# Linear attention with a gated feed-forward layer on one core: how the reciprocal denominators get from 72 partitions to 128

## The chip, the core and the metric

The kernel runs on one core of one Trainium2 chip. The metric is the device time of one execution in microseconds (us), the median of three runs. The engines are TensorE (PE in the profile, with PEld for its weight loads), VectorE (DVE), ScalarE (ACT), GpSimd (POOL) and SyncE (SP), whose queue issues all of this kernel's transfers.

## What is computed

The reference has two parts. Cut to what matters:

```python
def phi(x):                                    # x: batch 8, heads 8, 576 positions, 64 dims
    proj = einsum('bhsd,df->bhsf', x, w_phi)   # 128 features
    proj = proj - max(abs(proj), axis=-1)
    return concatenate([exp(proj), exp(-proj)], axis=-1)
q_p, k_p = phi(q), phi(k)
kv  = einsum('bhsf,bhsd->bhfd', k_p, v)
z   = sum(k_p, axis=2)
num = einsum('bhsf,bhfd->bhsd', q_p, kv)
den = einsum('bhsf,bhf->bhs', q_p, z)[..., None] + 1e-06
x = num / den                                  # 512 wide per position, all heads side by side
h = maximum(x @ w_in, 0)                       # 1024 wide
h_out = (h * sigmoid(conv(h, conv_w, 3 taps along the positions))) @ w_out
```

The change concerns one step of it, the division `num / den`.

## The kernel before, in words

The work is done batch by batch (b = 0 to 7). The eight heads of a batch are four pairs (p = 0 to 3), and a pair lies on 128 partitions: 64 dims of one head above 64 dims of the other. For each pair of pairs (qd = 0, 1) and each of five groups of positions (g = 0 to 4) there is a chain for k and a chain for q.

- `k_process` loads k and v, splits k into two float32r parts (`kxh`, `kxl`, on POOL), projects (`kp`), takes the maximum (`km`) and subtracts it (`ks`) on DVE, exponentiates on ACT (`ke`) and accumulates `kv` on PE.
- `q_process` does the like for q (`qxh`, `qxl`, `qp`, `qm`, `qs`), transposes (`tp`), exponentiates (`qh`, `qe`, `ql`), and multiplies with `kv` (`nm`). The product has 65 rows: 64 of the numerator and one of the denominator. ACT copies the numerators to `num` (128 x 576 for a pair) and the denominator row to `dr`; a transfer spreads `dr` over 72 partitions of 16 numbers each (`den`, line 377).
- `x_process` divides, once for each pair. DVE adds 1e-6 and takes the reciprocal (`rc`, 72 x 16, lines 392 and 393). Four transfers of line 397 bring each head's 576 reciprocals to two single partitions of the constant tile `rr` (partitions 0 and 32 for one head, 64 and 96 for the other). Then, for each of two halves c of the positions (290 wide, overlapping at the middle), a DVE stream shuffle spreads partition 0 of each block of 32 over its block (`xf`, line 405), a DVE multiplication forms num / den (line 406), ACT rounds it to float32r (`xh`) and DVE takes the rest (`xl`, both by way of `split`, lines 60 and 65).
- `h_part` and `o_part` are the feed-forward layer: `hp` (line 429) multiplies `xh`, `xl` with `win_hi`, `win_lo`; ACT applies relu (`h`); `conv_process` makes the three-tap convolution, the sigmoid and the gate on POOL, DVE and ACT (`c`, `gh`, `gl`); `op` (line 488) multiplies with `wout_hi`, `wout_lo`, and the output is stored from `os`.
- In the first part of the run the weights are loaded too: `w_r` holds 64-bit floats, and DVE, ACT and POOL turn them into float32r pairs (`w_t`, lines 96 to 105).

The order of the instructions on each engine is not the order of the code. A planner at the end of the function decides in which sequence the chains are recorded, and after that a scheduler orders each engine's instructions by priority and by its own estimate of when operands are ready. So an edit in `x_process` moves instructions on every engine. On each engine, and on SP's queue, instructions then run strictly in that order: one that waits holds up all behind it.

Of the kernel before, what the change touches and what calls it, by code (L numbers as in the profile page):

```python
# [7 lines left out]
F32 = mybir.dt.float32  # L8
# [4 lines left out]
ALU = mybir.AluOpType  # L13
AX = mybir.AxisListType.X

B, H, S, D = 8, 8, 576, 64
F = 128
DM, FF = 512, 1024
P = 128
NQ = 2  # L20
TC = 288
HW = TC + 2
# [13 lines left out]
def kernel(  # L36
# [13 lines left out]
    nc = tc.nc  # L50
    cp = ctx.enter_context(tc.tile_pool(name="cp", bufs=1))
    sb = ctx.enter_context(tc.tile_pool(name="sb", bufs=1))
    pg = ctx.enter_context(tc.tile_pool(name="pg", bufs=4, space=bass.MemoryType.PSUM))
    pm = ctx.enter_context(tc.tile_pool(name="pm", bufs=2, space=bass.MemoryType.PSUM))
    pk = ctx.enter_context(tc.tile_pool(name="pk", bufs=1, space=bass.MemoryType.PSUM))

    def split(src, hi, lo, eng_hi, eng_lo):

        if eng_hi is nc.scalar:
            nc.scalar.activation(out=hi, in_=src, func=AF.Copy)  # L60
        elif eng_hi is nc.gpsimd:
            nc.gpsimd.tensor_scalar(out=hi, in0=src, scalar1=1.0, scalar2=0.0, op0=ALU.mult, op1=ALU.add)  # L62
        else:
            nc.vector.tensor_copy(out=hi, in_=src)
        eng_lo.tensor_tensor(out=lo, in0=src, in1=hi.bitcast(F32), op=ALU.subtract)  # L65
# [12 lines left out]
    split(wbd_f, wbd_hi, wbd_lo, nc.vector, nc.vector)  # L78
    idn = load_const(ident, [P, P], "idn")


    rr = cp.tile([P, S], F32, name="rr")
    nc.gpsimd.memset(rr, 0.0)

# [66 lines left out]
    def pe(ns):  # L153
        return ("pe", ns)
# [4 lines left out]
    def until(*keys):  # L159
        return ("until", [k for k in keys if k is not None])  # L160

    def set_ready(key, ns=0):
        ready[key] = now[0] + ns * LAT
# [134 lines left out]
    xh, xl = {}, {}  # L298

    def q_process(b, qd, g):  # L300
# [80 lines left out]
        if g == 2 or g == 4:  # L381
            spawn(x_process(b, qd * 2 + g // 2 - 1))

    def x_process(b, p):
        yield ("wait", 4000)
        qd, pr = divmod(p, 2)
        dn, nt = den[b, qd, pr], numt[b, qd, pr]
        if 4 * b + p > 0:
            yield until(("x", *divmod(4 * b + p - 1, 4), 1))
        with tc.high_priority():  # L390
            rc = sb.tile([72, 16], F32, name=f"rc{b}_{p}", tag="rc", bufs=2)
            nc.vector.tensor_scalar(out=dn, in0=dn, scalar1=1e-6, scalar2=None, op0=ALU.add)
            nc.vector.reciprocal(out=rc, in_=dn)
            for i in range(2):
                for j in range(2):
                    row = D * i + 32 * j
                    nc.sync.dma_start(out=rr[row : row + 1, :].rearrange("o (r c) -> o r c", c=16),
                                      in_=rc.rearrange("(r i) c -> i r c", i=2)[i])
        yield ("wait", 4500)
        for c in range(2):  # L400
            yield until(("h", 2 * (b - 1) + c) if b > 0 else None)
            t0 = 0 if c == 0 else S - HW
            with tc.high_priority():
                xf = sb.tile([P, HW], F32, name=f"xf{b}_{p}_{c}", tag="xf", bufs=2)
                nc.vector.stream_shuffle(out=xf, in_=rr[:, t0 : t0 + HW], mask=[0] * 32)
                nc.vector.tensor_tensor(out=xf, in0=nt[:, t0 : t0 + HW], in1=xf, op=ALU.mult)
                xh[b, p, c] = sb.tile([P, HW], F32R, name=f"xh{b}_{p}_{c}", tag="xh", bufs=8)
                xl[b, p, c] = sb.tile([P, HW], F32R, name=f"xl{b}_{p}_{c}", tag="xl", bufs=8)
                split(xf, xh[b, p, c], xl[b, p, c], nc.scalar, nc.vector)
            set_ready(("x", b, p, c), 2500)  # L410
            yield pe(125)

# [145 lines left out]
    while moe is not None or chains or active:  # L558
        while chains and sum(1 for p in active if p[2]) < WINDOW:
            b, x, g, kind = chains.pop(0)  # L560
# [3 lines left out]
            p = active[-1]  # L564
# [10 lines left out]
        if can_a and (a_first or not can_m):  # L575
            p = active[can_a[0]]
# [66 lines left out]
```

## Time and profile before

| | |
|---|---|
| median of 3 runs | 825.59 us (824.98 to 825.75) |
| the profiled execution's own time | 825.6 us |
| its span, first to last instruction | 823.5 us |
| PE busy | 788.0 us, 96% of the span |
| DVE busy | 645.6 us, 78% |
| ACT busy | 569.5 us, 69% |
| POOL busy | 307.6 us, 37% |
| granted TensorE clock, mean | 0.989 |
| stream shuffles (line 405) | 64, 29.0 us of DVE |
| multiplications num / den (line 406) | 64, 32.0 us of DVE |
| transfers of line 397 | 128, of 2.2 KB each |

Busy shares are averages over the whole run. The kernel has a first part of about 140 us, in which weights are converted beside the first batches, and then a repeating part with a period of about 95.7 us for each batch; the two have to be read apart, by stretches of time. A row of the view by stretches has, for each engine, its busy us and in brackets the number of instructions, then the granted clock, the mean busy share of the 16 DMA engines and the GB/s they moved. A row of the view by lines has the line, engine, operation, tiles and shapes, the count, the busy us and the mean ns of one, and the idle time just before with what ended it.

### The profile page before, as it was taken

The page shows a single profiled execution, that of the slowest core. Times are in us where ns is not written, and L with a number is a line of the kernel's source. Part 1 is how long each engine was busy: PE and PEld are TensorE (multiplying, and loading weights), DVE is VectorE, ACT ScalarE, POOL GpSimd, SP SyncE. Part 2 cuts the span into 40 slices and gives each one's busy share as a digit, 9 for nine tenths or more (in the row PEclk, how much of TensorE's full clock was granted, in tenths as well). Part 3 has the DMA queues.
Part 4 walks back from the last instruction along what each step waited for, and adds up shares of the span by engine and source line. Part 5 has one row for each costly group of instructions (what it writes and reads, how often), then busy time and mean ns, then how long its engine had stood idle before and what let it go on. Part 6 is the DMA issues. An engine that isn't in the chain of part 4 may idle for free.

```text
span 823.5 us, 17817 instructions
## 1 busy us (share of the span) xinstructions
PE 788.0 (96%) x6350; PEld 772.5 (94%) x6350; DVE 645.6 (78%) x1390; ACT 569.5 (69%) x1228; POOL 307.6 (37%) x467
## 2 busy tenths in 40 slices
PE   7778779999999999999999999999999999999998
PEld 6767678999999999999999999999999999999998
DVE  4879999799987769787779878788697878766551
ACT  4598777797788867687586857678576867644332
POOL 4757765444443424414233333424334131111110
PEclk9799989999999999999999999999999999999999
DMA  6544421211211302121121211112021100000001
GB/s 187 157 134 135 135 66 47 67 41 44 70 56 44 93 18 71 27 82 50 46 61 43 69 34 60 47 50 82 15 77 29 56 12 19 13 30 30 23 23 44
DMA packets 56328, 49.18 MB, mean 60 GB/s; under 512 B 15024, under 2 KB 54192, under 8 KB 56240
## 3 DMA queue, kind: packets, MB, share of 16 engines
q1 hardware_dynamic: 56240, 48.05, 20.1%
q8 instruction: 51, 0.84, 0.4%
q14 instruction: 37, 0.30, 0.1%
HBM read 38.13 MB, written 9.44 MB: 58 GB/s over the span
## 4 chain that ended last, share of the span: by engine, by line
PE 74%; DVE 10%; ACT 7%; issue 4%; DMA 3%; POOL 1%; SPq 1%; DVEq 0%; ACTq 0%; POOLq 0%
PE op L488 22%; PE hp L429 21%; PE kv L255 8%; PE nm L356 8%; PE tp L320 3%; PE kp L199 2%; PE nm L348 2%; PE kp L200 2%; PE kp L201 2%; PE qp L199 1%; PE qp L200 1%; PE qp L201 1%; DMA w_r<-in_w_in_dram 1%; PE kv L251 1%; DVE qm L204 1%
## 5 line engine op out<-in xcount | busy, mean ns | idle before, releaser
L457 DVE SCALAR_TENSOR_TENSOR c<-h,cw,c 128x287 f32<-128x287 f32 (+1 forms) x256 | 138.7, 554 | 49.4 <-POOL c L452 47.5
L452 POOL TENSOR_SCALAR c<-h,cw 128x288 f32<-128x288 f32 x128 | 75.0, 588 | 243.6 <-ACT h L436 184.3
L255 PE MATMUL kv<-v,ke 128*128 128x65 f32 x1024 | 159.4, 255 | 1.4 <-ACT ke L236 1.2
L255 PEld LDWEIGHTS kv<-v,ke 128*128 128x128 f32 x1024 | 153.5, 193 | 4.8 <-ACT ke L236 1.8
L429 PE MATMUL hp<-xh,win_hi 128*128 128x290 f32 x512 | 153.2, 300 | 0.6 <-ACT os L493 0.6
L429 PE MATMUL hp<-xl,win_hi 128*128 128x290 f32 x512 | 152.7, 298 | 0.2 <-DVE xl L65 0.2
L488 PE MATMUL op<-gh,wout_hi 128*128 128x288 f32 x512 | 152.2, 298 | 0.0
L429 PE MATMUL hp<-xh,win_lo 128*128 128x290 f32 x512 | 151.9, 297 | 0.0
L488 PE MATMUL op<-gl,wout_hi 128*128 128x288 f32 x512 | 151.4, 296 | 0.0
L488 PE MATMUL op<-gh,wout_lo 128*128 128x288 f32 x512 | 150.9, 295 | 0.0
L436 ACT ACTIVATE h<-hp 128x290 f32<-128x290 f32 x128 | 52.2, 414 | 71.7 <-PE hp L429 71.2
L429 PEld LDWEIGHTS hp<-xh,win_hi 128*128 128x128 f32 x512 | 96.7, 190 | 1.5 <-ACT os L493 1.4
L62 POOL TENSOR_SCALAR kxh<-kr 128x256 fp32r<-128x256 f32 (+1 forms) x80 | 43.8, 547 | 144.1 <-PE kp L200 134.6
L429 PEld LDWEIGHTS hp<-xl,win_hi 128*128 128x128 f32 x512 | 97.0, 189 | 0.6 <-DVE xl L65 0.6
L429 PEld LDWEIGHTS hp<-xh,win_lo 128*128 128x128 f32 x512 | 97.1, 190 | 0.0
L488 PEld LDWEIGHTS op<-gh,wout_lo 128*128 128x128 f32 x512 | 96.4, 188 | 0.0
L488 PEld LDWEIGHTS op<-gl,wout_hi 128*128 128x128 f32 x512 | 96.2, 188 | 0.0
L488 PEld LDWEIGHTS op<-gh,wout_hi 128*128 128x128 f32 x512 | 96.1, 188 | 0.0
L65 DVE TENSOR_TENSOR ql<-qe,qh 128x512 fp32r<-128x512 f32 x112 | 79.9, 732 | 9.9 <-ACT qh L60 9.5
L236 ACT ACTIVATE ke<-ks 128x512 f32<-128x512 f32 (+1 forms) x80 | 46.9, 586 | 39.1 <-DVE ks L206 36.5
L326 ACT ACTIVATE qe<-tp 128x512 f32<-128x512 f32 x112 | 61.2, 595 | 12.2 <-PE tp L320 10.4
L356 PE MATMUL nm<-ql,kvh 128*65 128x256 f32 x224 | 68.4, 308 | 0.3 <-DVE ql L65 0.2
(84 smaller groups left out, 1989.5 us busy)
## 6 DMA issues: line engine op xcount, KB each, us to landing
v<-in_vt_dram SPq DMA_DIRECT2D x80, 130.0 KB
out_dram<-os SPq DMA_DIRECT2D x64, 144.0 KB
qr<-in_qT_dram SPq DMA_DIRECT2D x64, 128.0 KB
kr<-in_kT_dram SPq DMA_DIRECT2D x64, 128.0 KB
w_r<-in_w_in_dram SPq DMA_DIRECT2D x8, 512.0 KB
w_r<-in_w_out_dram SPq DMA_DIRECT2D x8, 512.0 KB
rr<-rc SPq DMA_DIRECT2D x128, 2.2 KB
qr<-in_qT_dram SPq DMA_DIRECT2D x16, 64.0 KB
```

Of the source, the lines that this page charges most:

```text
L62: nc.gpsimd.tensor_scalar(out=hi, in0=src, scalar1=1.0, scalar2=0.0, op0=ALU.mult, op1=ALU.add)
L65: eng_lo.tensor_tensor(out=lo, in0=src, in1=hi.bitcast(F32), op=ALU.subtract)
L199: nc.tensor.matmul(out=o, lhsT=his, rhs=wbd_hi, start=True, stop=False)
L236: nc.scalar.activation(out=e[:, 0], in_=pr, func=AF.Exp)
L255: ins = nc.tensor.matmul(out=kp[i][:, s, p0 : p0 + VW], lhsT=lhsT, rhs=v[:, (2 * t + i) * VW : (2 * t + i + 1) * VW], start=False, stop=(g ...
L326: nc.scalar.activation(out=e, in_=tp.rearrange("p i t s -> p i (t s)"), func=AF.Exp, scale=1.0 - 2.0 * s)
L356: ins = after(ins, lambda: nc.tensor.matmul(out=ps[:, i, o : o + w], lhsT=w_, rhs=x_, start=(k == 0), stop=(k == 5)))
L429: nc.tensor.matmul(out=ps, lhsT=w_, rhs=x_, start=(k == 0), stop=(k == 11))
L436: nc.scalar.activation(out=hs, in_=ps, func=AF.Relu)
L452: nc.gpsimd.tensor_scalar(out=cv, in0=hs[:, o : o + TC], scalar1=cw[:, f, 1:2], scalar2=0.0, op0=ALU.mult, op1=ALU.add)
L457: nc.vector.scalar_tensor_tensor(out=cv[:, lo:hi], in0=hs[:, o + j - 1 + lo : o + j - 1 + hi], scalar=cw[:, f, j : j + 1], in1=cv[:, lo:hi ...
L488: nc.tensor.matmul(out=ps, lhsT=w_, rhs=x_, start=(k == 0), stop=(k == 23))
```

## The change

The reciprocals take another way from the 72 partitions of `rc` to the 128 partitions of the pair. One transfer writes them to a tile `rd` in device memory, two rows of 576. A second transfer reads them back with each row repeated over 64 partitions into `rb` (128 x 576). The constant tile `rr`, its memset, the stream shuffles and the tile `xf` are gone. The multiplication with `num` is done once for the pair over all 576 positions, in place in `rb`, in the first of the two halves; both halves then split from slices of `rb`. `rb` and `rd` have two buffers each.

```diff
+    dp = ctx.enter_context(tc.tile_pool(name="dp", bufs=2, space=bass.MemoryType.DRAM))
...
-    rr = cp.tile([P, S], F32, name="rr")
-    nc.gpsimd.memset(rr, 0.0)
...
             nc.vector.reciprocal(out=rc, in_=dn)
-            for i in range(2):
-                for j in range(2):
-                    row = D * i + 32 * j
-                    nc.sync.dma_start(out=rr[row : row + 1, :].rearrange("o (r c) -> o r c", c=16),
-                                      in_=rc.rearrange("(r i) c -> i r c", i=2)[i])
+            rd = dp.tile([2, S], F32, name=f"rd{b}_{p}", tag="rd", bufs=2)
+            nc.sync.dma_start(out=rd.rearrange("i (r c) -> r i c", c=16), in_=rc)
+            rb = sb.tile([P, S], F32, name=f"rb{b}_{p}", tag="rb", bufs=2)
+            nc.sync.dma_start(out=rb, in_=rd.unsqueeze(1).broadcast_to([2, D, S]))
         yield ("wait", 4500)
         for c in range(2):
...
-                xf = sb.tile([P, HW], F32, name=f"xf{b}_{p}_{c}", tag="xf", bufs=2)
-                nc.vector.stream_shuffle(out=xf, in_=rr[:, t0 : t0 + HW], mask=[0] * 32)
-                nc.vector.tensor_tensor(out=xf, in0=nt[:, t0 : t0 + HW], in1=xf, op=ALU.mult)
+                if c == 0:
+                    nc.vector.tensor_tensor(out=rb, in0=nt, in1=rb, op=ALU.mult)
...
-                split(xf, xh[b, p, c], xl[b, p, c], nc.scalar, nc.vector)
+                split(rb[:, t0 : t0 + HW], xh[b, p, c], xl[b, p, c], nc.scalar, nc.vector)
```

The new code moves instructions. On DVE, the rows from the first pair's reciprocal (`rc_0`) to the first use of what the transfers bring (for batch 0; `w_t` are weights being converted, `km`, `ks`, `qm`, `qs` maxima and differences of the next groups). Before:

```order
L393 RECIPROCAL rc_0_829<-den_0_0_500 72x16
L98 TENSOR_SCALAR w_t<-w_r 128x512
L100 SCALAR_TENSOR_TENSOR w_t<-w_r,w_t 128x512
L204 TENSOR_REDUCE km_0_0_711<-kp_0_0_707 128x2
L103 SCALAR_TENSOR_TENSOR w_t<-w_t,w_r 128x512
L204 TENSOR_REDUCE qm_1_1_721<-qp_1_1_718 128x4
L206 TENSOR_TENSOR ks_0_0_713<-kp_0_0_707,km_0_0_711 128x256
L96 TENSOR_SCALAR w_t<-w_r 128x512
L206 TENSOR_TENSOR qs_1_1_723<-qp_1_1_718,qm_1_1_721 128x512
L204 TENSOR_REDUCE qm_1_2_736<-qp_1_2_733 128x4
L405 STREAM_SHUFFLE xf_0_0_948<-rr 128x290
```

The same place after the change, where the first use is the multiplication into `rb`:

```order
L391 RECIPROCAL rc_0_829<-den_0_0_500 72x16
L96 TENSOR_SCALAR w_t<-w_r 128x512
L98 SCALAR_TENSOR_TENSOR w_t<-w_r,w_t 128x512
L202 TENSOR_REDUCE km_0_0_711<-kp_0_0_707 128x2
L101 SCALAR_TENSOR_TENSOR w_t<-w_t,w_r 128x512
L202 TENSOR_REDUCE qm_1_1_721<-qp_1_1_718 128x4
L204 TENSOR_TENSOR ks_0_0_713<-kp_0_0_707,km_0_0_711 128x256
L403 TENSOR_TENSOR rb_0_834<-num_0_0_501,rb_0_834 128x576
L94 TENSOR_SCALAR w_t<-w_r 128x512
L204 TENSOR_TENSOR qs_1_1_723<-qp_1_1_718,qm_1_1_721 128x512
```

The first use has moved forward past three instructions: nine stood between it and the reciprocal, six stand there now. For the four pairs of batch 0 the numbers between are 9, 10, 9 and 13 before, and 6, 7, 7 and 12 now.

On PE, the place at which the first feed-forward products of batch 0 (`hp`, from `xh_0_0`) stand among the attention's products (`nm`, `kv`, `tp`, `kp`, `qp`). Before:

```order
L255 MATMUL kv_1_1_439<-v_1_4_599,ke_1_4_698 128x65 x2
L320 MATMUL tp_1_1_800<-idn,qs_1_1_723 128x128
L199 MATMUL kp_0_1_808<-wbd_hi,kxh_0_1_727 128x256
L200 MATMUL kp_0_1_808<-wbd_lo,kxh_0_1_727 128x256
L201 MATMUL kp_0_1_808<-wbd_hi,kxl_0_1_728 128x256
L199 MATMUL kp_0_1_808<-wbd_hi,kxh_0_1_727 128x256
L200 MATMUL kp_0_1_808<-wbd_lo,kxh_0_1_727 128x256
L201 MATMUL kp_0_1_808<-wbd_hi,kxl_0_1_728 128x256
L320 MATMUL tp_1_1_800<-idn,qs_1_1_723 128x128 x3
L196 MATMUL qp_1_3_822<-wbd_f,qr_1_3_760 128x256 x2
L348 MATMUL nm_1_0_850<-qh_1_0_704,kvh_1_0_794 65x64
```

(Nine more rows of `nm_1_0` and `kv_0` follow there before the first `hp`.) After the change:

```order
L346 MATMUL nm_0_4_764<-qh_0_4_684,kvh_0_1_436 65x256
L253 MATMUL kv_1_1_439<-v_1_4_599,ke_1_4_698 128x65 x2
L426 MATMUL hp_0_1578<-xh_0_0_949,win_hi_93 128x290
L426 MATMUL hp_1_1593<-xh_0_0_949,win_hi_93 128x290
L318 MATMUL tp_1_1_800<-idn,qs_1_1_723 128x128
L197 MATMUL kp_0_1_808<-wbd_hi,kxh_0_1_727 128x256
L198 MATMUL kp_0_1_808<-wbd_lo,kxh_0_1_727 128x256
L199 MATMUL kp_0_1_808<-wbd_hi,kxl_0_1_728 128x256
```

The first two `hp` products have moved ahead of `tp_1_1`, `kp_0_1`, `qp_1_3` and `nm_1_0`, which now stand behind them.

## The prediction

> **What bounds the kernel now.** I read the stretches of time first, because a mean over the run mixes two regimes. PE, PEld, DVE, ACT and POOL busy, then clock, DMA share, GB/s:
>
> ```profile
> span 823.5 us, 17817 instructions
> 57.00:140.00 83.00, 67.88 (x518) 61.05 (x517) 81.45 (x153) 64.23 (x139) 57.97 (x67) 0.96 0.35 104
> 175.00:250.00 75.00, 74.02 (x622) 73.79 (x623) 71.33 (x158) 60.83 (x130) 35.07 (x49) 1.00 0.18 50
> 300.00:395.70 95.70, 95.64 (x803) 95.22 (x800) 77.05 (x169) 69.12 (x150) 33.39 (x57) 1.00 0.19 53
> ```
>
> From 300 us on, one period of 95.70 us has 95.64 us of PE: nothing but PE counts there, and DVE is idle for 18.65 us of each period. Between 57 and 140 us it is the other way round: DVE is busy for 81.45 of 83 us and PE for 67.88, so PE loses 15.1 us there. That is where weights are converted on DVE beside the first batches, and where the four divisions of batch 0 lie. Between 175 and 250 us both are nearly full. So a saving or a delay on DVE counts at full price before 140 us, perhaps in part up to 250 us, and hardly at all after that.
>
> Then the waits, of PE and of DVE in 57 to 140 us (total, times, longest), with one row of the whole run's waits:
>
> ```profile
> PE tp L320 <- DVE ks L206: 4.0, 3, 3.4
> DVE w_t L96 <- POOL wout_lo L65: 0.8, 1, 0.8
> DVE xf L405 <- DMA rr<-rc: 15.6, 7, 3.7
> ```
>
> PE's longest wait there is on DVE. DVE's longest is 0.8 us, and none of the shuffles' waits for `rr` falls into that stretch: all seven (15.6 us) come later, where DVE has room. So the reciprocals' way through the transfers is hidden behind other DVE work today, and the question is whether it still is.
>
> **What the change takes off DVE.** The lines of DVE in 57 to 140 us:
>
> ```profile
> L65 DVE TENSOR_TENSOR ql<-qe,qh 128x512 fp32r<-128x512 f32 x10 | 10.6, 1070 | 0.0
> L206 DVE TENSOR_TENSOR ks<-kp,km 128x512 f32<-128x512 f32 (+1 forms) x12 | 7.3, 608 | 0.0
> L204 DVE TENSOR_REDUCE qm<-qp 128x4 f32<-128x512 f32 (+1 forms) x12 | 7.6, 630 | 0.0
> L103 DVE SCALAR_TENSOR_TENSOR w_t<-w_t,w_r 128x512 f32<-128x512 int32 x9 | 7.1, 789 | 0.0
> L406 DVE TENSOR_TENSOR xf<-num,xf 128x290 f32<-128x290 f32 x10 | 7.1, 748 | 0.0
> L100 DVE SCALAR_TENSOR_TENSOR w_t<-w_r,w_t 128x512 int32<-128x512 int32 x9 | 6.9, 771 | 0.0
> L204 DVE TENSOR_REDUCE km<-kp 128x4 f32<-128x512 f32 (+1 forms) x11 | 6.9, 624 | 0.0
> L98 DVE TENSOR_SCALAR w_t<-w_r 128x512 int32<-128x512 int32 x9 | 5.9, 651 | 0.3 <-ACT w_t L97 0.3
> L96 DVE TENSOR_SCALAR w_t<-w_r 128x512 int32<-128x512 int32 x9 | 5.1, 570 | 0.8 <-POOL wout_lo L65 0.8
> L405 DVE STREAM_SHUFFLE xf<-rr 128x290 f32<-128x290 f32 x10 | 4.3, 482 | 0.0
> ```
>
> For each pair two shuffles (2 x 482 ns) and two multiplications (2 x 748 ns) go, 2460 ns, and one multiplication of 576 columns comes. No row shows it. Between the 290 columns of line 406 (748 ns) and the 512 of `ql` (1070 ns) a column costs 1.45 ns, which gives 1163 ns at 576; its bounds are 1070 ns and twice 748 ns. I take 1163: 1.3 us saved for each pair, 5.2 us in batch 0 (3.9 to 5.6). The 28 later pairs save as much each, where PE doesn't wait for it: nothing, as long as DVE's idle time stays. The memset that goes ran on POOL before anything needed it, and the splits keep their sizes: nothing.
>
> **What the change makes of the transfers.** Before, four transfers are issued one behind the other, and the shuffle waits for the last. The chain of work that ended last shows such a case undisturbed, and early in the run a slow landing of a load (start, us, what):
>
> ```profile
> 8.01 2.57 DMA kr<-in_kT_dram
> ...
> 253.04 0.75 SPq L397
> 253.84 0.71 SPq L397
> 254.59 1.83 DMA rr<-rc
> ```
>
> An issue takes 0.7 to 0.8 us, and a transfer 1.83 us from its issue to landing; the four take 4.2 us. Now there are two that depend on each other: the write to `rd`, and the read, which SP may only issue when the write has landed. The write moves the same 72 rows of 64 bytes and I give it the same 1.83 us (no row shows it alone; the bounds are 1.83 and the 2.57 of the slow load). The read moves 128 rows of 2304 bytes, 295 KB, and its price hangs on how many of the 16 DMA engines carry it. For that, the packets of the page and all the issues (count, KB each):
>
> ```profile
> DMA packets 56328, 49.18 MB, mean 60 GB/s; under 512 B 15024, under 2 KB 54192, under 8 KB 56240
> v<-in_vt_dram SPq DMA_DIRECT2D x80, 130.0 KB
> out_dram<-os SPq DMA_DIRECT2D x64, 144.0 KB
> qr<-in_qT_dram SPq DMA_DIRECT2D x64, 128.0 KB
> kr<-in_kT_dram SPq DMA_DIRECT2D x64, 128.0 KB
> w_r<-in_w_in_dram SPq DMA_DIRECT2D x8, 512.0 KB
> w_r<-in_w_out_dram SPq DMA_DIRECT2D x8, 512.0 KB
> rr<-rc SPq DMA_DIRECT2D x128, 2.2 KB
> qr<-in_qT_dram SPq DMA_DIRECT2D x16, 64.0 KB
> kr<-in_kT_dram SPq DMA_DIRECT2D x16, 64.0 KB
> den<-dr SPq DMA_DIRECT2D x64, 2.0 KB
> den<-dr SPq DMA_DIRECT2D x32, 0.5 KB
> wbd_f<-in_wbd_dram SPq DMA_DIRECT2D x1, 128.0 KB
> idn<-in_ident_dram SPq DMA_DIRECT2D x1, 64.0 KB
> cw_raw<-in_conv_w_dram SPq DMA_DIRECT2D x1, 24.0 KB
> ```
>
> Data packets under 512 B are 128 x 36 of `rr`, 64 x 32 and 32 x 8 of `den` (64 bytes each) and the 128 of `cw_raw`: 7040. The other 7984 fit one closing packet from each engine that takes part. The issues are 547 transfers, so 16 engines for each would give 8752. The 768 that are missing are 128 x 4 + 32 x 8: the transfers of 36 rows use 12 engines and those of 8 rows use 8. So the engines are dealt out by the outermost count, as a divisor of it: 12 is the largest up to 16 that divides 36. The read has an outermost count of 128 on the side of `rb` and of 2 on the side of `rd` (two heads, each row then repeated 64 times). No transfer of before has two unequal sides, so 2 and 16 engines are both open, and this decides the forecast. I take 2, since an engine can only be dealt whole rows of the outer loop on both sides.
>
> The Trainium skill ("DMA: Bandwidth & Descriptors", "Why a DMA increments its semaphore by 16 and not by 1", and again in "Rules for kernel authors") states it so: the count is the largest up to 16 that divides the outermost size of both sides, and a broadcast with few copies outermost confines the whole transfer to so few engines. By that rule the change is slower; the trace agrees with it as far as the 12 and the 8 above.
>
> What one engine moves, from the densest stretch of weight loads:
>
> ```profile
> 35.00:37.00 2.00, 2.00 (x22) 2.00 (x20) 2.00 (x3) 0.48 (x1) 1.68 (x2) 1.00 0.71 251
> ```
>
> 251 GB/s over 0.71 x 16 engines is 22.1 GB/s for each. Half of 295 KB is 147.5 KB, 6.7 us on each of two engines; on 16 it would be 0.8 us. With 1.83 us for issue and landing the read takes 8.5 us, and write and read 10.4 us (2.7 and 4.5 us on 16 engines).
>
> From the Trainium skill's figure of about 27 GiB/s for an engine (the same page, "Specifications") one would estimate 5.1 us in place of 6.7, and a forecast lower by 6.4 us; no row here shows an engine at that rate.
>
> **What that costs.** The multiplication stands in DVE's queue where the order puts it: 6, 7, 7 and 12 instructions behind the reciprocal in batch 0, together 32. They are of the seven kinds of rows quoted above (570 to 789 ns), 0.66 us each in the mean, so 21.2 us of work. Four times 10.4 us less 21.2 us leaves 20.4 us in which DVE waits, about 6 us for each of the first three pairs and 2 for the fourth. Behind the multiplication wait `w_t`, `qs_1_1`, `qm_1_2` and `xl`, and behind those ACT and PE. On PE the first `hp` now stands ahead of `tp_1_1` and `kp_0_1` and holds them up until `xh_0_0` is there, so PE has no other work to turn to. On SP the read waits 1.1 us past the write's issue; queued behind it are `v_0_2`, `kr_0_4`, `qr_1_3` and a `den`. Each of these is on all 16 engines, so its share on the two slow ones lands up to 6.7 us later. I price that at nothing for batch 0, because DVE stands still in that time anyway; it is the reason for a rival below. SP itself issues 64 transfers fewer, and is idle enough for that to bring nothing.
>
> DVE in this stretch is idle for 1.55 us, which can be absorbed. The sum: -5.2 + 20.4 - 1.6 = +13.6 us. For batches 1 and 2 (42 and 43 instructions between) there are waits too, but PE is served ahead there. An instruction of 175 to 250 us is 71.33/158 = 0.45 us, so in batch 1 the waits are 41.6 - 18.9 = 22.7 us against 5 us saved and 3.7 us of idle. I take zero for it, with a bound of 14 us. The reason is this stretch around a shuffle that waited 3.7 us without PE losing more than 0.03:
>
> ```profile
> 250.00:260.00 10.00, 9.97 (x87) 9.81 (x85) 5.47 (x15) 7.97 (x18) 4.08 (x8) 1.00 0.26 70
> ```
>
> From batch 3 on only the last pair of a batch has its multiplication close (7 to 13 instructions), about 5 us of waiting against 18.65 us of idle: nothing.
>
> **The sum.** The profiled execution took 825.6 us, 2.1 us more than its span, and the median of the runs is 825.59, so no correction is needed: 825.6 + 13.6 = 839.2 us. Bounds of this case: with 789 or 570 ns for each of the 32 instructions between, the waits are 16.4 or 23.4 us and the time 835.2 or 842.2; a write that lands in 2.57 us adds 4 x 0.74 = 3.0, so 835 to 845.
>
> **Rivals.**
> - Sixteen engines (chance 0.13). If the 128 rows of `rb` decide, write and read take 4.5 us, no more than the four transfers today, and fit behind the 21.2 us of other work but for about 0.5 us. DVE's 5.2 us then count in full where DVE is the bound: 825.6 - 5.2 + 0.5 = 820.9 us, faster. For it: every 128-row transfer of before runs on 16. Against it: the 2 on the other side.
> - Two engines, but the waits cost PE little (0.12): PE turns out to have work ahead in batch 0 as it has at 250 us. Then waits and savings nearly cancel: about 825.5 us, from 824 to 828. Against it: PE's 15.1 us of idle time before 140 us.
> - The slow read also blocks others (0.15): batch 1 pays its waits less savings and idle, and loads behind the read come late for POOL. About 839.2 + 14 = 853 us. For it: 71.33 of 75 us of DVE. Against it: the reserve at 250 us.
> - The forecast, 0.60.
>
> About 0.2% (1.7 us) is what a measurement of this kernel can tell from no change. Slower by more: 0.57 of the main case, 0.15, and 0.05 of the second rival, 0.77. Faster: 0.11 of the first, 0.02 of the second and 0.01, 0.14. The same: 0.09. The range from 823 to 850 leaves out the first rival's middle and most of the third.
>
> **What would show it.** Right: reads of `rb` that land 8 to 9 us after their issue, two closing packets for each; waits of DVE's line 403 on `rb` of about 20 us before 150 us; more idle time of PE before about 155 us, and then the same period of 95.7 us. Wrong: reads that land in under 3 us, or waits of that size beside an unchanged idle time of PE; or periods longer than 95.7 us, which would be the third rival.

## The result, and the profile after

| | before | after |
|---|---|---|
| median of four runs | 825.38 us (824.98 to 825.75) | 974.16 us (971.47 to 977.13) |
| ratio | | 1.1803, 95% interval 1.1768 to 1.1839 |
| span of the profiled execution | 823.5 us | 969.7 us |
| PE busy / idle in the span | 788.0 / 35.5 us | 839.4 / 130.3 us |
| DVE busy | 645.6 us | 616.2 us |
| granted TensorE clock, mean | 0.989 | 0.926 |

The change costs 148.8 us, where 13.6 us were forecast, so the direction was right and the size was not. The times of the span add up: PE's idle time grew by 94.8 us, and PE was busy for 51.4 us longer with the same 6350 matmuls.

First, which engines carried the new read. The page after, packets and queue rows, then the read's issue:

```profile
DMA packets 57030, 58.45 MB, mean 60 GB/s; under 512 B 11632, under 2 KB 50800, under 8 KB 56944
rb<-rd SPq DMA_DIRECT2D x32, 288.0 KB
rd<-rc SPq DMA_DIRECT2D x32, 4.5 KB
```

The count is made as for before. Data packets under 512 B are 72 x 32 for `rd`, 2304 for `den` and 128 for `cw_raw`, 4736 together, so 6896 are closing packets. There are 483 transfers, 16 each would be 7728, and 832 are missing: 256 for `den`'s transfers of 8 rows, 32 x 4 for `rd` on 12 engines, and 32 x 14 for `rb`. The read runs on two engines. (The view counts 1024 bytes to a KB: its 288.0 KB are the 295 KB of the prediction.)

Next, DVE's waits for that read: over the whole run, from 57 to 140 us (batch 0), and from 700 to 790 us (batch 6) (total, times, longest):

```profile
DVE rb L403 <- DMA rb<-rd: 170.2, 32, 7.5
```

```profile
DVE rb L403 <- DMA rb<-rd: 21.1, 4, 6.4
```

```profile
DVE rb L403 <- DMA rb<-rd: 23.5, 4, 6.0
```

All 32 multiplications wait, 5.3 us each. The four of batch 0 wait 21.1 us, as forecast (20.4). The four of batch 6 wait 23.5 us, where the forecast had about 5 for a late batch and called them free. The stretches of time show what that did to PE (columns as in the prediction):

```profile
57.00:140.00 83.00, 57.17 (x356) 49.93 (x355) 58.33 (x95) 52.71 (x112) 42.67 (x51) 0.83 0.37 107
300.00:396.00 96.00, 82.81 (x655) 80.83 (x655) 61.73 (x128) 60.72 (x130) 26.17 (x43) 0.95 0.22 59
396.00:492.00 96.00, 89.07 (x716) 88.44 (x714) 58.15 (x118) 59.34 (x125) 33.24 (x53) 0.96 0.22 59
588.00:684.00 96.00, 83.07 (x648) 82.24 (x647) 60.59 (x121) 57.77 (x120) 28.26 (x49) 0.91 0.21 59
```

Read the matmul counts. Before, a period of 95.7 us held 803 matmuls and next to no idle time of PE; now 96 us hold 648 to 716, with a clock below 1. The loss by stages follows from equal numbers of matmuls, first before and then after:

```profile
0.00:140.00 140.00, 110.57 (x788) 99.50 (x789) 119.89 (x222) 99.79 (x211) 91.28 (x112) 0.94 0.42 126
0.00:396.00 396.00, 364.83 (x2935) 352.30 (x2936) 332.02 (x688) 295.33 (x636) 191.93 (x271) 0.98 0.27 79
396.00:684.00 288.00, 287.86 (x2408) 286.43 (x2408) 230.33 (x505) 208.08 (x452) 98.92 (x165) 1.00 0.17 49
```

```profile
0.00:163.00 163.00, 122.45 (x786) 110.12 (x787) 115.07 (x194) 100.41 (x212) 88.38 (x112) 0.86 0.40 117
0.00:471.00 471.00, 391.93 (x2935) 374.67 (x2936) 321.26 (x611) 296.57 (x636) 188.41 (x272) 0.92 0.28 77
0.00:817.00 817.00, 700.29 (x5342) 680.60 (x5343) 539.80 (x1060) 506.90 (x1090) 284.10 (x434) 0.92 0.23 66
```

The 788 matmuls that before had done by 140 us were done at about 163 us: 23 us late. The 2935 of 396 us came at about 471 us: 75 late. The 5343 of 684 us came at about 817 us: 133 late. So the loss isn't a matter of the first 140 us. After these it grows by about 19 us for every period of 95.7 us, up to 684 us, and by 13 us in what is left.

### The profile page after: what moved, and what is told of

It reads as the page before. It is cut to its first block, busy times and chain, and to the rows that moved or that the text cites. A ratio compares the mean times of both kernels' runs of the same rounds, so it can differ in the third digit from the quotient of the medians.

```text
span 969.7 us, 17565 instructions
## 1 busy us (share of the span) xinstructions
PE 839.4 (87%) x6350; PEld 817.7 (84%) x6350; DVE 616.2 (64%) x1230; ACT 572.6 (59%) x1228; POOL 303.3 (31%) x466
## 4 chain that ended last, share of the span: by engine, by line
PE 40%; DMA 30%; DVE 18%; ACT 6%; issue 4%; POOL 1%; SPq 0%; ACTq 0%; DVEq 0%; POOLq 0%
DMA rb<-rd 22%; PE hp L426 15%; PE op L485 8%; PE nm L354 5%; PE kv L253 5%; DMA den<-dr 4%; DVE c L454 3%; DVE c L462 2%; PE tp L318 2%; DMA rd<-rc 2%; DVE ql L66 2%; DVE qm L202 2%; DMA w_r<-in_w_in_dram 2%; DVE rb L403 2%; DVE ks L204 1%
## 5 line engine op out<-in xcount | busy, mean ns | idle before, releaser
L426 PE MATMUL hp<-xh,win_hi 128*128 128x290 f32 x512 | 157.8, 310 | 18.0 <-ACT xh L61 8.6
L454 DVE SCALAR_TENSOR_TENSOR c<-h,cw,c 128x288 f32<-128x288 f32 (+1 forms) x256 | 141.6, 562 | 46.3 <-POOL c L449 43.4
L253 PE MATMUL kv<-v,ke 128*128 128x65 f32 x1024 | 170.0, 266 | 0.7 <-ACT ke L234 0.4
L253 PEld LDWEIGHTS kv<-v,ke 128*128 128x128 f32 x1024 | 165.7, 207 | 5.2 <-ACT ke L234 1.7
L449 POOL TENSOR_SCALAR c<-h,cw 128x288 f32<-128x288 f32 x128 | 80.4, 630 | 246.9 <-ACT h L433 212.7
L426 PE MATMUL hp<-xh,win_lo 128*128 128x290 f32 x512 | 155.8, 304 | 0.0
L485 PE MATMUL op<-gh,wout_lo 128*128 128x288 f32 x512 | 154.5, 302 | 0.0
L403 DVE TENSOR_TENSOR rb<-num,rb 128x576 f32<-128x576 f32 x32 | 25.1, 785 | 170.2 <-DMA rb<-rd 170.2
L63 POOL TENSOR_SCALAR kxh<-kr 128x256 fp32r<-128x256 f32 (+1 forms) x80 | 40.2, 503 | 234.8 <-PE kp L198 225.3
L66 DVE TENSOR_TENSOR ql<-qe,qh 128x512 fp32r<-128x512 f32 x112 | 82.1, 748 | 29.4 <-ACT qh L61 29.4
L318 PE MATMUL tp<-idn,qs 128*128 128x128 f32 x288 | 69.2, 303 | 25.2 <-DVE qs L204 22.4
## 6 DMA issues: line engine op xcount, KB each, us to landing
rb<-rd SPq DMA_DIRECT2D x32, 288.0 KB
```

What stands on the lines that cost most here:

```text
L253: ins = nc.tensor.matmul(out=kp[i][:, s, p0 : p0 + VW], lhsT=lhsT, rhs=v[:, (2 * t + i) * VW : (2 * t + i + 1) * VW], start=False, stop=(g ...
L318: nc.tensor.transpose(out=tp[:, i, t, :], in_=pr[:, 2 * t + i, :], identity=idn)
L403: nc.vector.tensor_tensor(out=rb, in0=nt, in1=rb, op=ALU.mult)
L426: nc.tensor.matmul(out=ps, lhsT=w_, rhs=x_, start=(k == 0), stop=(k == 11))
L449: nc.gpsimd.tensor_scalar(out=cv, in0=hs[:, o : o + TC], scalar1=cw[:, f, 1:2], scalar2=0.0, op0=ALU.mult, op1=ALU.add)
L454: nc.vector.scalar_tensor_tensor(out=cv[:, lo:hi], in0=hs[:, o + j - 1 + lo : o + j - 1 + hi], scalar=cw[:, f, j : j + 1], in1=cv[:, lo:hi ...
```

## The experiments

Three theories stood at the start. **A**, held buffers: the product lies in `rb` and keeps one of its two buffers until the last split, so a read starts late. **B**, length: the read takes 8.5 us and its use is queued too few DVE instructions behind it, so DVE stands still and everything queued behind it waits too. **C**, a crowded pair of engines: the read holds up other transfers that need the same two engines.

| kernel | us (lowest to highest) | ratio to before | 95% interval |
|---|---|---|---|
| after | 974.16 (971.47 to 977.13) | 1.1803 | 1.1768 to 1.1839 |
| product in place | 971.54 (969.52 to 972.33) | 1.1767 | 1.1749 to 1.1785 |
| four engines | 894.04 (886.95 to 896.67) | 1.0812 | 1.0762 to 1.0863 |
| sixteen engines | 837.87 (834.45 to 841.8) | 1.0153 | 1.0118 to 1.0188 |
| sixteen, in place | 842.7 (842.32 to 843.83) | 1.0208 | 1.0191 to 1.0225 |
| two, in place, late use | 861.82 (857.5 to 864.57) | 1.0425 | 1.0387 to 1.0463 |
| sixteen, in place, late use | 830.62 (829.1 to 832.51) | 1.0052 | 1.0034 to 1.0069 |
| before + unused reads, early | 988.52 (986.25 to 989.98) | 1.1974 | 1.1953 to 1.1995 |
| before + unused reads, per pair | 901.25 (900.3 to 901.71) | 1.0905 | 1.0885 to 1.0926 |
| before, one shuffle and one multiplication | 835.94 (835.5 to 837.15) | 1.0119 | 1.0099 to 1.0138 |
| the same, late use | 830.76 (828.24 to 832.29) | 1.0057 | 1.0031 to 1.0083 |

Before, run beside them, took 825.44, 826.06 and 826.59 us in the three groups of runs.

### Product in place: are the buffers held?

```diff
-                    nc.vector.tensor_tensor(out=rb, in0=nt, in1=rb, op=ALU.mult)
+                    nc.vector.tensor_tensor(out=nt, in0=nt, in1=rb, op=ALU.mult)
...
-                split(rb[:, t0 : t0 + HW], xh[b, p, c], xl[b, p, c], nc.scalar, nc.vector)
+                split(nt[:, t0 : t0 + HW], xh[b, p, c], xl[b, p, c], nc.scalar, nc.vector)
```

> The changed kernel took 974.2 us; DVE waited for the read of rb 32 times, 170 us together. Here the product is written in place into num instead of rb, so rb is free right after the multiplication and no read has to wait for a buffer; the read stays one transfer on two engines. Theory A (held buffers: the two rb buffers are kept until the second half is split, so reads are issued late): the waits for rb fall to those of the first batches, 20 to 40 us, and the time to 835 to 850 us. Theory B (length: a read of 8.4 us stands a few DVE instructions ahead of its use, in whatever order, because the scheduler reckons it short; in this kernel's order 4 to 11 instructions stand between for every pair): 32 waits of about 5 us stay, 940 to 990 us. Theory C (the slow reads hold up the other transfers on the same two engines): as B.

Measured: 971.54 us. DVE's waits in this kernel:

```profile
DVE num L403 <- DMA rb<-rd: 193.8, 32, 8.8
```

The waits didn't shrink, they grew from 170.2 to 193.8 us. Held buffers are real, as the part on the prediction shows, but freeing them doesn't help: every read is now issued 1.9 to 3.5 us after its write, and its use stands only 0 to 11 DVE instructions behind that issue. Theory A falls.

### Sixteen engines, with the product in `rb` and in place

```diff
-            nc.sync.dma_start(out=rb, in_=rd.unsqueeze(1).broadcast_to([2, D, S]))
+            for i in range(2):
+                nc.sync.dma_start(out=rb[D * i : D * i + D, :], in_=rd[i : i + 1, :].broadcast_to([D, S]))
```

> The read is cut in two, one of 64 rows for each head, so that the outermost count is 64 on both sides and 16 engines carry it; all else is as in the changed kernel, the held buffers too. Theory A: reads from the fourth batch on are still issued late and DVE still waits for most of them, some 3 us each: 870 to 920 us. Theory B: each read lands in under 3.5 us, the waits fall under 40 us together, 816 to 832 us. Theory C: as B.

> Both edits: 16 engines for the reads and the product in place in num. All theories: 815 to 830 us; if it is clearly below the one with 16 engines alone, the held buffers cost that difference (A has a share), otherwise they cost nothing once the read is short.

Measured: 837.87 and 842.7 us, 6 and 13 us above the most that theory B allowed, and far below the 870 of theory A. The page of the first has 515 transfers and these packets:

```profile
DMA packets 57990, 58.46 MB, mean 70 GB/s; under 512 B 12592, under 2 KB 51760, under 8 KB 57904
```

and DVE's waits in it are

```profile
DVE rb L404 <- DMA rb<-rd: 35.1, 23, 3.0
```

Less the 4736 data packets, 7856 closing packets are left of 8240, and the 384 that are missing are those of `den` and `rd` alone: the read runs on sixteen engines. DVE's waits fall from 170.2 to 35.1 us, and 136 of the 149 us are gone. The bytes, the path through device memory and the single multiplication are all still there. So the two engines are the cause of nine tenths of the loss. Putting the product in place on top of it brought nothing here either: it was 5 us slower.

### Four engines: does the loss follow the read's duration?

The reciprocals are written twice, as four rows, so that the read's outer count is 4:

```diff
-            rd = dp.tile([2, S], F32, name=f"rd{b}_{p}", tag="rd", bufs=2)
-            nc.sync.dma_start(out=rd.rearrange("i (r c) -> r i c", c=16), in_=rc)
+            rd = dp.tile([4, S], F32, name=f"rd{b}_{p}", tag="rd", bufs=2)
+            for k in range(2):
+                nc.sync.dma_start(out=rd.rearrange("(i k) (r c) -> k r i c", k=2, c=16)[k], in_=rc)
...
-            nc.sync.dma_start(out=rb, in_=rd.unsqueeze(1).broadcast_to([2, D, S]))
+            nc.sync.dma_start(out=rb, in_=rd.unsqueeze(1).broadcast_to([4, D // 2, S]))
```

> The changed kernel with the reciprocals written to device memory twice, as four rows, so that the read has 4 on its outer side and should run on four engines: a quarter of 295 KB at 22.1 GB/s is 3.3 us in place of 6.7, the read lands in about 5.2 us in place of 8.5, and the second write adds one issue (0.75 us). If the loss follows the time of the read (12 us over before at 0.8 us on an engine, 149 us at 6.7), it is about 12 + 137 x (3.3 - 0.8) / (6.7 - 0.8) = 70 us, so 895 us, with waits of DVE for rb of 80 to 110 us. If most of the loss comes from the slower clock of PE behind long stalls, shorter stalls cost less than their share: 850 to 870 us. If sixteen engines helped only because the transfer was cut in two, the time stays near 970 us.

Measured: 894.04 us, where a loss that follows the read's duration gave 895. The packets, and DVE's waits:

```profile
DMA packets 59782, 58.60 MB, mean 66 GB/s; under 512 B 14384, under 2 KB 53552, under 8 KB 59696
```

```profile
DVE rb L404 <- DMA rb<-rd: 97.8, 32, 6.1
```

515 transfers again, 7040 data packets under 512 B (`rd` twice as many), 7344 closing ones of 8240: 896 are missing, 256 for `den`, 64 x 4 for `rd`, 32 x 12 for `rb`. So four engines. With 2, 4 and 16 engines DVE waits 170.2, 97.8 and 35.1 us, and the loss is 149, 67 and 12 us.

### Late use: does it matter where the multiplication stands in DVE's queue?

The multiplication is queued behind a later subtraction of line 204, and the planner waits longer before it records the rest of the pair. 24 to 79 DVE instructions then lie between reciprocal and multiplication, but 17 for the third pair from the end and 6 to 9 for the last two. The two edits were made together; how much each does wasn't tried. Against the kernel with the product in place:

```diff
-        nc.vector.tensor_tensor(out=pr, in0=ps3, in1=m.unsqueeze(2).broadcast_to([P, 2 * n, F]), op=ALU.subtract)
+        late[0] = nc.vector.tensor_tensor(out=pr, in0=ps3, in1=m.unsqueeze(2).broadcast_to([P, 2 * n, F]), op=ALU.subtract)
...
-        yield ("wait", 4500)
+        yield ("wait", 8000)
...
-                    nc.vector.tensor_tensor(out=nt, in0=nt, in1=rb, op=ALU.mult)
+                    after(late[0], lambda: nc.vector.tensor_tensor(out=nt, in0=nt, in1=rb, op=ALU.mult))
```

> The kernel with the product in place in num (971.5 us) and the read still one transfer on two engines, but the multiplication is queued on DVE behind a subtraction of a later group: 24 to 79 DVE instructions stand between reciprocal and multiplication, in place of 4 to 11 (only the last two pairs have 6 and 7). Theory B (the read is long and its use is queued too early, so DVE stands still): DVE's waits for rb fall from 194 us to under 25 us and the time to 818 to 840 us, with the slow read unchanged. Theory C (the slow reads hold up the other transfers): the waits for rb go, but those for k, q, v, den and the output stay, and so does at least a third of the loss, 870 us or more.

> Sixteen engines for the read, product in place, and the multiplication queued late as above. Theory B: no wait for rb worth naming, the saved DVE time stands alone: 814 to 826 us. Theory C: the same, and below the one with two engines by what the slow reads cost others.

Measured: 861.82 us on two engines, between the ranges of the two theories, and 830.62 us on sixteen, 5 us above that of theory B. DVE's waits for the transfers in the late kernel on two engines:

```profile
DVE den L391 <- DMA den<-dr: 31.1, 14, 6.8
DVE num L404 <- DMA rb<-rd: 13.8, 2, 7.1
```

The 32 waits for `rb` became 2, those of the last two pairs. With the product in place in all four kernels, the runs make a square (us):

| | two engines | sixteen engines |
|---|---|---|
| early use | 971.5 | 842.7 |
| late use | 861.8 | 830.6 |

With an early use the two engines cost 129 us, with a late one 31. And late use brings 110 us where the read is slow, but 12 where it is fast. So about 98 us exist only where a slow read meets an early use: DVE standing still at the head of its queue, theory B. The 31 us remain though hardly anything waits for `rb` itself. About 11 of them are lost with the last two pairs (13.8 us of waits against 3.8 on sixteen engines): the 5600th matmul starts 27.6 us later than before, at 746 us, and the 5800th 39.1 us later. For the rest, some 20 us, theory C is left: DVE's waits for `den` are 31.1 us here and 7.8 us in the late kernel on sixteen engines. The next runs try it by itself.

### Unused reads: what does the slow read cost others?

Both kernels keep before's way for the reciprocals and add reads whose result nothing uses. The first reads the same two rows each time, so nothing holds the reads back:

```diff
+    rd = dp.tile([2, S], F32, name="rd", tag="rd", bufs=1)
+    nc.sync.dma_start(out=rd, in_=rr[0:2, :])
...
+            rb = dp.tile([P, S], F32, name=f"rb{b}_{p}", tag="rb", bufs=2)
+            nc.sync.dma_start(out=rb, in_=rd.unsqueeze(1).broadcast_to([2, D, S]))
```

> The kernel before, with shuffles and all, and beside it for each pair a read of the same 128 rows from two rows of device memory on two engines, whose target is a device-memory tile that nobody uses. The result does not depend on it. It prices what the slow reads do to the other transfers alone. Theory C: at least a third of the 149 us, 870 to 930 us. Theories A and B: the other transfers have room, 825 to 845 us.

Measured: 988.52 us, outside both ranges and no price for C. The scheduler put the reads, which depend on nothing, ahead of almost all other work. SP's queue and PE in that stretch:

```profile
34.98 7.30 SPq L403 DMA_DIRECT2D rb<-rd  x1
42.38 5.51 SPq L182 DMA_DIRECT2D kr<-in_kT_dram  x1
47.93 0.61 SPq L403 DMA_DIRECT2D rb<-rd  x1
48.64 5.26 SPq L182 DMA_DIRECT2D kr<-in_kT_dram  x1
```

```profile
80.00:100.00 20.00, 2.26 (x8) 1.81 (x8) 0.00 (x0) 0.00 (x0) 1.88 (x4) 0.50 0.15 57
100.00:120.00 20.00, 0.00 (x0) 0.00 (x0) 0.00 (x0) 0.00 (x0) 0.00 (x0) 0.50 0.24 81
```

PE did nothing for 20 us. Issues on SP took 5 to 7 us, and what depends on the loads waited: DVE up to 79.1 us for a `den`, POOL up to 28.7 us for a `kr`. The run shows how reads queued on two engines hold up SP, and nothing on the changed kernel. The second kernel ties each read to its own pair's reciprocal:

```diff
+            rd = dp.tile([2, S], F32, name=f"rd{b}_{p}", tag="rd", bufs=2)
+            nc.sync.dma_start(out=rd.rearrange("i (r c) -> r i c", c=16), in_=rc)
+            ru = dp.tile([P, S], F32, name=f"ru{b}_{p}", tag="ru", bufs=2)
+            nc.sync.dma_start(out=ru, in_=rd.unsqueeze(1).broadcast_to([2, D, S]))
```

> The kernel before, and beside its own four transfers for each pair also the write of the reciprocals to device memory and the read of them on two engines at the place where the changed kernel has it, into device memory that nobody uses; the result does not depend on them. Unlike the first kernel of this kind, whose reads depended on nothing and were all queued into the first 200 us, each read here waits for its own pair's write. Theory C: 870 us or more. Theory B: the others have room for it, 825 to 845 us.

Measured: 901.25 us, 75 us over before, though no engine needs what the read brings. What waits is work whose own transfers are issued after it; before, then this kernel:

```profile
DVE den L392 <- DMA den<-dr: 9.8, 12, 2.2
ACT dr L374 <- DMA den<-dr: 1.8, 4, 0.9
```

```profile
DVE den L393 <- DMA den<-dr: 58.1, 15, 8.7
ACT dr L375 <- DMA den<-dr: 54.6, 16, 7.9
```

The transfers of `den` are 0.5 or 2.0 KB, and DVE waits up to 8.7 us for one now. In the chain of work that ended last such a transfer takes this long from its issue to its landing, before and then in this kernel (start, us, what):

```profile
119.89 1.72 DMA den<-dr
```

```profile
61.20 7.80 DMA den<-dr
```

So theory C holds too: other transfers land late because of the read. That SP itself waits for the new write before it issues the read isn't the reason: it did so for 17.5 us here and for 26.8 us in the late kernel on sixteen engines, which lost 5 us. The price of theory C hangs on what is queued behind the read, some 20 us in the late kernel and up to 75 here, where the added transfers also moved the order of the instructions, so no one number for its share in the changed kernel can be given.

### One shuffle and one multiplication, without device memory

With sixteen engines 12 us are left over before, 5 with late use, which the slow read can't explain. These two kernels keep the four transfers to `rr`, and do one shuffle and one multiplication of 576 columns for each pair, in the second with the shuffle queued late as above:

```diff
-                xf = sb.tile([P, HW], F32, name=f"xf{b}_{p}_{c}", tag="xf", bufs=2)
-                nc.vector.stream_shuffle(out=xf, in_=rr[:, t0 : t0 + HW], mask=[0] * 32)
-                nc.vector.tensor_tensor(out=xf, in0=nt[:, t0 : t0 + HW], in1=xf, op=ALU.mult)
+                if c == 0:
+                    xf = sb.tile([P, S], F32, name=f"xf{b}_{p}", tag="xf", bufs=1)
+                    nc.vector.stream_shuffle(out=xf, in_=rr, mask=[0] * 32)
+                    nc.vector.tensor_tensor(out=nt, in0=nt, in1=xf, op=ALU.mult)
...
-                split(xf, xh[b, p, c], xl[b, p, c], nc.scalar, nc.vector)
+                split(nt[:, t0 : t0 + HW], xh[b, p, c], xl[b, p, c], nc.scalar, nc.vector)
```

> The kernel before with its four transfers into rr, but one shuffle of 576 columns and one multiplication in place in num for each pair. It is the part of the change that thins out DVE, without the way through device memory. By both theories it lies within 819 to 827 us: DVE is freed of 10 to 25 us, of which 2 to 5 us stand where DVE is the bound. Above 830 us the earlier use of the result, or the order, would cost something that neither theory has.

> The kernel before with one shuffle of 576 columns and one multiplication in place for each pair (835.94 us, +10 over before, with nothing in device memory), and that shuffle now queued late: 26 to 81 instructions of DVE behind the reciprocal in place of 2 to 12, as in the late kernel with sixteen engines. What is left of the loss without a slow read is told apart here. If it is the early place of the use in DVE's queue (the shuffle then waits for the last of four transfers, 4.2 us), late use takes most of the 10 us back: 826 to 829 us, and DVE's waits for rr go. If it is the one wide operation itself (it holds DVE 0.8 us longer in one piece, and both halves' splits come behind it), the time stays at 834 to 838 us.

Measured: 835.94 us, and 830.76 us with late use, between the two ranges for it. The first lies above the range of both theories. DVE was busy for 650.0 and 645.0 us, against 645.6 before, so it wasn't freed as expected. Joining the two halves costs about 10 us by itself, without any device memory, and late use, with which DVE's waits for `rr` fall from 12.6 to 2.0 us, takes half of that back. The other 4 us stay open.

The 4.6 us of the best kernel on sixteen engines can be followed one step further. That kernel has DVE busy for 617.7 us (before 645.6), its PE is idle for 35.5 us as before, and it is slower all the same: PE is busy 4.6 us longer for the same matmuls. Its stretch from 57 to 140 us has a granted clock of 0.91 where before has 0.96:

```profile
57.00:140.00 83.00, 70.91 (x527) 65.10 (x526) 76.06 (x128) 66.98 (x148) 57.80 (x68) 0.91 0.40 122
```

In the trace's record of the clock, PE works for 31.1 us of that kernel's run at a clock of 0.50, and for 13.6 us of before's. At half speed that is 8.7 us more lost, enough for the difference. Why its clock falls more often wasn't tried. No version beat the kernel before.

## Why the prediction was right or wrong, step by step

**Right: two engines, and the durations.** The count of closing packets confirms two engines, and with the other kernels four and sixteen. The Trainium skill's rule ("DMA: Bandwidth & Descriptors", "Why a DMA increments its semaphore by 16 and not by 1") agrees with all three counts. The chain of work that ended last, after, shows the first write and read and one later read (start, us, what):

```profile
51.84 2.39 DMA rd<-rc
54.24 8.95 DMA rb<-rd
...
359.67 13.54 DMA rb<-rd
```

In that chain reads take 8.02 to 8.95 us from issue to landing, or 12.4 to 13.9 where one follows close behind another; writes take 1.90 to 2.39. The forecast had 8.5 and 1.83. The rate from the row of weight loads (22.1 GB/s for an engine) served. The Trainium skill's figure of about 27 GiB/s (the same page, "Specifications") gives an estimate of 5.1 + 1.8 = 6.9 us, and no read of that chain landed in under 8.02.

**Right: the waits of batch 0, but not their price.** 20.4 us forecast, 21.1 measured, in four waits. The count of instructions between was the right measure there, since the read could start as soon as its write had landed. The forecast loss was 13.6 us, and 23 were lost. By the rows above PE's idle time for the first 786 matmuls grew by 11 us, near the forecast, and PE's busy time for them by another 12 us, at a mean clock of 0.86 in place of 0.94; the forecast has no term for that.

**Wrong, and decisive: "From batch 3 on only the last pair of a batch has its multiplication close (7 to 13 instructions), about 5 us of waiting against 18.65 us of idle: nothing."** Two things in this step failed. The first is the count. Here are the rows of DVE and SP around pairs 0 and 1 of batch 3, the first batch of which the step speaks, after (start, us, what):

```profile
337.88 0.24 DVE L391 RECIPROCAL rc<-den 72x16 f32<-72x16 f32 x1
...
357.48 0.83 DVE L66 TENSOR_TENSOR xl<-rb,xh 128x290 fp32r<-128x290 f32 x2
...
359.56 1.06 DVE L454 SCALAR_TENSOR_TENSOR c<-h,cw,c 128x288 f32<-128x288 f32 x2
367.08 0.76 DVE L403 TENSOR_TENSOR rb<-num,rb 128x576 f32<-128x576 f32 x1 [6.46 <-DMA rb<-rd]
373.23 0.76 DVE L403 TENSOR_TENSOR rb<-num,rb 128x576 f32<-128x576 f32 x1 [5.39 <-DMA rb<-rd]
```

```profile
338.95 0.82 SPq L394 DMA_DIRECT2D rd<-rc  x1
351.98 0.82 SPq L394 DMA_DIRECT2D rd<-rc  x1
358.33 1.85 SPq L396 DMA_DIRECT2D rb<-rd  x2
```

Pair 0's reciprocal was done at 338.1 us and its write issued at 339.0. 37 instructions lie between it and its multiplication, and by that count the read is long done. But the read was issued at 358.3 us only: there are two buffers `rb`, and the splits that free them (`xl` of earlier pairs) run from 357.5 on. From the read's issue to its use there are five instructions, about 2 us of work, and DVE stood for 6.46 and then, for pair 1, 5.39 us. In the changed kernel 17 of the 32 reads are issued 5 to 28 us after their write in this way, where the others follow it by 2 to 4 us. What counts is the distance from the read's issue to its use, not from the reciprocal. And with the buffers free, as in the kernel with the product in place, the scheduler puts the use 4 to 13 instructions behind the reciprocal in every pair, so that the waits are as long by another way. The distance is short by whichever route.

The second is the cover. The 18.65 us of idle time that DVE has in a period didn't pay for a wait in one piece. While DVE stands, `qs`, `km`, `ql` and the `xl` behind it aren't made, and PE runs out of work within the wait. PE's waits for them over the run, after:

```profile
PE tp L318 <- DVE qs L204: 22.4, 7, 6.3
PE nm L354 <- DVE ql L66: 19.2, 6, 5.1
```

Idle time in a mean over a period is no reserve against one wait of 6 us; the reserve is how much work lies ready in front of PE, and of that the prediction had one sample, a single wait of 3.7 us.

**Wrong for the same reason: "I take zero for it, with a bound of 14 us"** for batches 1 and 2. From 140 to 300 us of before's time, in which these two lie, about 35 us were lost: the 2134 matmuls of 300 us came at 358 us. The row at 250 us, on which the zero rested, showed PE surviving one wait of 3.7 us, and the new waits are 3.3 to 7.5 us, one for each pair.

**Left out: a slower clock behind each stall.** These are stretches of 2 us, after, around the second of the waits above:

```profile
370.00:372.00 2.00, 2.00 (x19) 2.00 (x18) 0.00 (x0) 0.00 (x0) 0.00 (x0) 1.00 0.66 161
372.00:374.00 2.00, 0.59 (x5) 0.35 (x3) 0.77 (x2) 0.00 (x0) 0.00 (x0) 1.00 0.13 46
374.00:376.00 2.00, 0.00 (x0) 0.00 (x0) 2.00 (x6) 1.00 (x3) 0.00 (x0) 0.79 0.28 74
376.00:378.00 2.00, 0.00 (x0) 0.00 (x0) 2.00 (x5) 1.96 (x3) 0.00 (x0) 0.50 0.19 66
378.00:380.00 2.00, 1.12 (x6) 1.15 (x6) 1.34 (x3) 0.07 (x1) 0.00 (x0) 0.50 0.03 9
380.00:382.00 2.00, 2.00 (x11) 2.00 (x11) 0.00 (x0) 0.71 (x2) 0.02 (x1) 0.51 0.00 0
382.00:384.00 2.00, 2.00 (x18) 2.00 (x18) 1.82 (x3) 2.00 (x6) 1.72 (x4) 1.00 0.00 0
```

PE runs dry at about 372.6 us. The mean of 0.79 in 374 to 376 us puts the fall of its clock to 0.50 at about 375.2, and there it stays until 382: in 380 to 382 us PE is busy all the time and makes 11 matmuls where it makes 18 to 20 at full clock. So this wait cost its own length and then some 3 us at half speed, of which half is lost. The record of the clock in the trace has 24 such stretches at 0.50 between 60 and 880 us, where before has one; the view by stretches sums them up (their length, then the busy us of each engine):

```profile
sum 133.20, PE 106.20 PEld 103.91 DVE 110.62 ACT 91.98 POOL 31.09; mean PE 4.43 PEld 4.33 DVE 4.61 ACT 3.83 POOL 1.30
```

With 8.3 us at the start of the run PE works for 114.5 us at half clock, and before for 13.6. Half of the 100.9 us more is 50.5, and PE's work took 51.4 us longer: the clock accounts for it. The Trainium skill ("TensorE: Matmul & The Clock Gate", "HAM oscillation — how this bites in real kernels") says that idle gaps of over about 3.4 us throttle TensorE to half. The rows agree in kind; here the clock fell some 2.6 us after PE ran dry, by ends of matmuls that the trace models. Six of the 24 stretches follow a last gap of 1.6 to 2.5 us, so the bound isn't a safe one here.

**Too small: the rival "The slow read also blocks others".** The mechanism is there (up to 75 us in the kernel with unused reads), but it was priced at 14 us, as a matter of batch 1.

**Not so: the rival "Sixteen engines" as a gain.** It said 820.9 us, and the kernel on sixteen engines took 837.9. Its wait of 0.5 us became 35.1 us in 23 waits, for the reason above: only 1 to 8 DVE instructions stand between the read's issue and its use. And where these waits were all but gone (3.8 us, late use) the time was 830.6 us, so the 5.2 us of saved DVE time didn't come out either.

**Sized wrong, without effect: the one multiplication.** Forecast 1163 ns. The group of line 403 on the page after has 785 (busy us, mean ns, then the idle time before):

```profile
L403 DVE TENSOR_TENSOR rb<-num,rb 128x576 f32<-128x576 f32 x32 | 25.1, 785 | 170.2 <-DMA rb<-rd 170.2
```

The 748 and 1070 ns from which it was worked out are means of a busy stretch; over the whole run the multiplications of 290 columns took 522 ns. DVE was busy for 29.4 us less over the run, and no stage of the changed kernel shows a gain from it.

## What to carry to other kernels

Before a transfer is put into a chain, count on how many engines it runs, by the outermost counts of both its sides; here 2, 4 and 16 engines were worth 149, 67 and 12 us of loss. Price a wait by the distance from the transfer's issue to its use, with the buffer that it needs in the account, and by what the waiting engine's queue holds up; mean idle time is no cover. And where the matmul engine would run dry for some 5 us, add what the time at half clock loses after that (here 51.4 us over the run, beside 94.8 us of idle time).

## What the runs showed of the hardware that was not expected

- In the stall shown, TensorE's granted clock fell to 0.50 some 2.6 us after PE ran dry, and stayed there for nearly 7 us, the first 3 us of new work among them. Over the 24 such stretches it fell 1 to 5 us after PE ran dry.
- A transfer of 0.5 to 2.0 KB issued behind a read of 295 KB on two engines kept DVE waiting for up to 8.7 us: the waits for `den` rose from 9.8 to 58.1 us.
- With several such reads under way, the issue of a load on SP took 5.26 and 5.51 us, where the median issue of that load is 0.35 us in the kernel before (1.71 at most). The issuing engine is held, and with it every transfer behind.
